# Program order on three engines, first loads in one queue by need, and a later router tail and x copy, in a gated linear-attention kernel

## The chip, the cores and the metric

The kernel runs on one core of one Trainium2 chip. The metric is device time in microseconds (us), lower is better. Times are medians of several executions. The granted TensorE clock of an execution is its mean over the span, 1 being full speed. In this kernel TensorE runs the matmuls (1510 instructions in the profile before), VectorE (278) and ScalarE (138) the element-wise work, POOL (GpSimd, 102) does small jobs and issues some copies, SP issues most copies (96 of 108 issues). PSUM is the memory that the matmuls write to; an evacuation takes a result out of it and frees its bank for the next matmuls (in the profile before, TensorE stood 2.85 us at the router for want of a bank). Warm-up matmuls are matmuls on zeros at the start, whose result is not used.

## The reference, cut to what matters

```python
qkv = x @ wqkv                                   # x: 2048 x 1024, wqkv: 1024 x 3072
pq, pk = phi(q), phi(k)                          # phi(t) = max(t,0) + min(exp(t),1) + 1e-6
kv, z = einsum(pk, v), pk.sum(rows)              # per head, 32 heads of 32
a = (pq @ kv / (pq @ z + 1e-6)) @ wo
r = x @ w_r; idx = argmax(r)                     # the router picks ONE row of x
y = (silu(x[idx] @ w_gate) * (x[idx] @ w_up)) @ w_down * sigmoid(r[idx])
b = x; b[idx] += y
g = sigmoid((x * gate_w).sum(-1))
out = g * a + (1 - g) * b
```

Nearly all work is dense projections. The one chain that is awkward is the router's: scores of all rows, the index of the largest, a fetch of that row from DRAM by a computed address, and a small feed-forward network on that one row, which is woven between the projections.

## The kernel before

The kernel is written in a framework that places instructions by a scheduler: the text of the program gives data dependences and rough priority, and the scheduler decides the order on each engine. The parts that the change and the argument touch (cuts marked with `# ...`):

```python
N_WARM = 8
load_x(0, 2); load_wkv(0); load_x(2, 2)          # tiles 0,1 ; first weight block ; tiles 2,3
# ... further weight blocks, transposed x, wq
nc.sync.dma_start(out=xp[:], in_=x2d)            # copy of x to a DRAM buffer that row idx will be patched in

def phi_evac(ps, out_ap):                        # evacuation of a PSUM bank; there are four
    nc.scalar.activation(e0[:], ps, ACTF.Exp)
    nc.vector.tensor_scalar(e1[:], e0[:], 1.0, EPS, op0=ALU.min, op1=ALU.add)
    nc.vector.scalar_tensor_tensor(out_ap, ps, 0.0, e1[:], op0=ALU.max, op1=ALU.add)
# ... router: scores, max, max_index on VectorE, then
nc.gpsimd.dma_start(out=c4[:], in_=cand[0:128:32, :])          # small copy across partitions
nc.vector.tensor_reduce(out=rmax[:], in_=c4[:, :, 0], ...)     # router tail: six small operations
# ...
idx_val = nc.values_load(idx_i[0:1, 0:1], engines=(POOL,), ...)
nc.gpsimd.dma_start(out=xsel_row[:], in_=x2d[bass.ds(idx_val, 1), :])   # the selected row
# ... in the feed-forward network, second half of the columns:
if nr < 4:
    nc.vector.memset(ps[96:128, :], 0.0)         # rows that no matmul of this half writes
# ... end of the key and value stage:
for i in range(3): nc.vector.tensor_copy(zcol[...], acc3[:, :, 128])
nc.vector.tensor_tensor(zc[:], mzc[:], zcol[...], op=ALU.mult)
for i in range(3): nc.vector.tensor_tensor(kvbd[...], acc3[...], mask_bd[...], op=ALU.mult)
rdA = den_group(0)                               # denominator: 16 matmuls on zc, banks freed by kvbd
```

## Time and profile before

| | before |
|---|---|
| median of 3 runs | 268.96 us (268.34 to 270.46) |
| profiled span | 267.3 us |
| TensorE busy | 255.7 us, 96% |
| idle in front of matmuls, summed | 8.2 us |
| mean granted clock, profiled run | 0.998 |

Three more from the page of the kernel before are needed later. The first is the granted clock in 40 equal slices of the span, in tenths, 9 being 90% or more. The other two are groups of instructions: line, engine, operation, count, then busy time, mean ns of one, and idle time before them.

```profile
PEclk9999999999999999999999999999999999999999
...
L195 PE MATMUL ps<-wkv,xT 128*128 128x512 bf16 x498 | 113.9, 379 | 2.2 <-DMA wkv<-in_A_wqkv_dram 1.0
...
L169 DVE TENSOR_SCALAR e<-e 128x512 f32<-128x512 f32 x64 | 31.4, 492 | 55.7 <-ACT e L167 55.5
```

After the start, where warm-up matmuls follow each other every 0.43 us and the clock records begin at 6.61 us, the clock stays at full speed (1.0 from 6.61 to 266.03 us) until the last matmul. The 379 ns of a projection matmul is the mean duration at that speed.

### The profile page before, as it was taken

Reading aid. Unit: us, or ns where it says so; the run is one execution under the profiler, and the core shown is the slowest. Engines: PE = TensorE matmul, PEld = TensorE weight load, DVE = VectorE, ACT = ScalarE, POOL = GpSimd, SP = SyncE. Lnnn points to the kernel's source line nnn. Section 1 sums busy time; section 2 is a strip of 40 time slices with the busy share of each in tenths; the row PEclk is TensorE's granted clock in tenths of the full one; section 3 lists DMA queues with packets and bytes.
Section 4 is the critical chain, followed back from the end, with each engine's and each line's share of the span. In section 5 each row is a group of like instructions: output and inputs, shape, how many; then the busy total and the mean of one; then the engine's idle time right before and its main releaser. Section 6 shows DMA issues by size and latency. Waiting matters only on the chain.

```text
span 267.3 us, 3972 instructions
## 1 busy us (share of the span) xinstructions
PE 255.7 (96%) x1510; PEld 121.8 (46%) x1537; DVE 144.5 (54%) x278; ACT 89.3 (33%) x138; POOL 50.3 (19%) x102
## 2 busy tenths in 40 slices
PE   7799999599999999999999999999999899999994
PEld 4444455245444445444444455544444344444443
DVE  4355014452375533539433425279999889984443
ACT  1433332123233322332322331233576623333310
POOL 7000001120000000000000000111969317990000
PEclk9999999999999999999999999999999999999999
DMA  6999998892078048019319608084000336455222
GB/s 228 359 312 220 246 521 306 292 415 93 0 259 333 1 154 316 4 45 348 120 36 357 238 0 300 17 286 168 1 1 2 125 100 197 150 170 177 86 78 78
DMA packets 33058, 47.71 MB, mean 178 GB/s; under 512 B 14152, under 2 KB 18640, under 8 KB 32976
## 3 DMA queue, kind: packets, MB, share of 16 engines
q1 hardware_dynamic: 32688, 47.32, 53.0%
q8 instruction: 12, 0.20, 0.3%
q0 software_dynamic: 320, 0.14, 0.2%
q14 instruction: 6, 0.05, 0.0%
q10 hardware_dynamic: 32, 0.00, 0.0%
HBM read 39.85 MB, written 8.39 MB: 180 GB/s over the span
## 4 chain that ended last, share of the span: by engine, by line
PE 77%; DVE 12%; DMA 7%; issue 2%; ACT 0%; POOL 0%; SPq 0%; DVEq 0%
PE ps L195 39%; PE ps L519 19%; PE ps L211 11%; DVE rb L476 4%; DVE e L169 3%; DMA c<-cand 3%; PE ps L320 3%; DVE pq_all L170 2%; DMA wkv<-in_A_wqkv_dram 2%; PE kvacc L204 2%; DMA rdp<-rd 1%; PE yps L359 1%; PE rps L237 1%; PE dps L453 1%; PE gl_ps L287 0%
## 5 line engine op out<-in xcount | busy, mean ns | idle before, releaser
L195 PE MATMUL ps<-wkv,xT 128*128 128x512 bf16 x498 | 113.9, 379 | 2.2 <-DMA wkv<-in_A_wqkv_dram 1.0
L195 PEld LDWEIGHTS <-xT 128*128 128x128 bf16 x512 | 48.8, 98 | 58.4 <-issue 2.9
L167 ACT ACTIVATE e<-ps 128x512 f32<-128x512 f32 x64 | 38.2, 597 | 81.7 <-PE ps L195 43.3
L169 DVE TENSOR_SCALAR e<-e 128x512 f32<-128x512 f32 x64 | 31.4, 492 | 55.7 <-ACT e L167 55.5
L211 PE MATMUL ps<-xT,wq 128*128 128x512 bf16 x248 | 58.3, 379 | 3.3 <-DVE idx_i L265 2.8
L519 PE MATMUL ps<-m_sb,pq_all 128*128 128x512 bf16 (+1 forms) x259 | 55.3, 372 | 1.0 <-DVE pq_all L170 0.6
L211 PEld LDWEIGHTS <-wq 128*128 128x128 bf16 x256 | 24.8, 98 | 33.6 <-issue 4.6
L519 PEld LDWEIGHTS <-pq_all 128*128 128x128 bf16 x264 | 25.7, 98 | 31.3 <-issue 1.8
L478 POOL TENSOR_TENSOR pq_all<-pq_all,rb 128x512 bf16<-128x512 bf16 x32 | 37.3, 1197 | 9.9 <-DVE rb L476 9.8
L200 ACT CAST vt<-ps 128x512 bf16<-128x512 f32 x32 | 18.8, 587 | 41.5 <-PE ps L195 41.5
L521 DVE SCALAR_TENSOR_TENSOR ot<-ps,gate,xg 128x512 bf16<-128x512 f32 (+1 forms) x33 | 23.8, 734 | 14.2 <-PE ps L519 14.1
L513 ACT ACTIVATE xg<-xt,omg 128x1024 f32<-128x1024 bf16 x16 | 18.2, 1151 | 29.7 <-DVE ot L521 25.0
L476 DVE STREAM_SHUFFLE rb<-rdp 128x512 f32<-128x512 f32 x32 | 22.7, 743 | 0.0
L170 DVE SCALAR_TENSOR_TENSOR pk<-ps,e 128x512 bf16<-128x512 f32 x32 | 22.1, 691 | 1.1
L170 DVE SCALAR_TENSOR_TENSOR pq_all<-ps,e 128x512 bf16<-128x512 f32 x32 | 21.8, 683 | 0.6
L192 POOL MEMSET vt<- 128x8 bf16 x16 | 1.9, 135 | 106.4 <-PE kvacc L204 106.4
L204 PEld LDWEIGHTS <-pk 128*128 128x128 bf16 x128 | 8.5, 98 | 3.3 <-issue 0.4
L204 PE MATMUL kvacc<-vt,pk 128*128 128x129 bf16 x128 | 9.7, 221 | 0.0
L484 ACT CAST m_sb<-ps 128x512 bf16<-128x512 f32 x16 | 8.6, 593 | 0.0
L458 DVE RECIPROCAL rd<-dn 128x512 f32<-128x512 f32 x2 | 6.7, 3353 | 3.2 <-ACT dn L456 3.2
L241 DVE CAST r_bf<-rps 128x512 bf16<-128x512 f32 x1 | 0.7, 691 | 13.9 <-PE rps L237 13.9
L365 POOL DMA_DIRECT2D xp<-brow x1 | 0.6, 575 | 38.5 <-DVE brow L364 38.5
(97 smaller groups left out, 87.0 us busy)
## 6 DMA issues: line engine op xcount, KB each, us to landing
wt<-in_B_w_down_dram SPq DMA_DIRECT2D x14, 512.0 KB, 9.2
wkv<-in_A_wqkv_dram SPq DMA_DIRECT2D x4, 1024.0 KB, 10.6
wt<-in_B_w_gate_dram SPq DMA_DIRECT2D x8, 512.0 KB, 21.6
wt<-in_B_w_up_dram SPq DMA_DIRECT2D x8, 512.0 KB, 8.1
xt<-xp SPq DMA_DIRECT2D x16, 256.0 KB, 2.7
out_dram<-ot SPq DMA_DIRECT2D x15, 256.0 KB, 2.0
wt<-in_B_w_gate_dram SPq DMA_DIRECT2D x8, 384.0 KB, 6.2
wt<-in_B_w_up_dram SPq DMA_DIRECT2D x8, 384.0 KB, 6.8
```

The source lines that it names most:

```text
L167: last_act[0] = nc.scalar.activation(e0[:], ps, ACTF.Exp)
L169: nc.vector.tensor_scalar(e1[:], e0[:], 1.0, EPS, op0=ALU.min, op1=ALU.add)
L170: nc.vector.scalar_tensor_tensor(out_ap, ps, 0.0, e1[:], op0=ALU.max, op1=ALU.add)
L195: nc.tensor.matmul(ps[:], lhsT=xT[:, c, t * P : (t + 1) * P], rhs=wkv[:, c, 512 * nb : 512 * nb + 512], start=(c == 0), stop=(c == KC - 1))
L200: nc.scalar.copy(vt_t[t][:, 4 * (nb - 2) : 4 * (nb - 2) + 4, 0:128], ps[:].rearrange("p (g e) -> p g e", g=4))
L204: nc.tensor.matmul(kv_slot(g), lhsT=pk_t[t][:, g * P : (g + 1) * P], rhs=vt_t[t][:, g, :], start=False, stop=False, skip_group_check=True)
L211: nc.tensor.matmul(ps[:], lhsT=wq[:, c, g * P : (g + 1) * P], rhs=xT[:, c, 512 * j : 512 * j + 512], start=(c == 0), stop=(c == KC - 1))
L476: nc.vector.stream_shuffle(rb[:], rd[:], [8 * (j % 2) + g] * 32)
L478: nc.gpsimd.tensor_tensor(sl, sl, rb[:], op=ALU.mult)
L513: pin_act(nc.scalar.activation(xg[:], xt[:], ACTF.Copy, scale=omg[:, t : t + 1]))
L519: nc.tensor.matmul(ps[:, 0:cw], lhsT=pq_all[:, g, t * P : (t + 1) * P], rhs=m_sb[:, g, c0 : c0 + cw], start=(g == 0), stop=(g == NG - 1))
L521: nc.vector.scalar_tensor_tensor(ot[:, c0 : c0 + cw], ps[:, 0:cw], gate[:, t : t + 1], xg[:, c0 : c0 + cw], op0=ALU.mult, op1=ALU.add)
```

## The change

The intent: fix the order by hand, so that a reduction that waits for a copy no longer stands in front of ready evacuations, and so that the first loads arrive in the order in which they are used. The core of the diff (cuts marked):

```diff
-N_WARM = 8
+N_WARM = 5
+    def in_order(engine, names):        # each instruction is pinned behind the last one on its engine
+        # ...
+    pe = in_order(nc.tensor, [...]);  dve = in_order(nc.vector, [...])
+    sp = in_order(nc.sync, [...]);    act = in_order(nc.scalar, [...])
# every nc.tensor / nc.vector / nc.scalar call below becomes pe / dve / act
-    load_x(0, 2)
-    load_wkv(0)
-    load_x(2, 2)
+    load_x(0, 1); load_w0(0); load_x(1, 1)
+    for c2 in range(1, 4): load_w0(c2)
+    load_x(2, 2)
# ...
-    nc.sync.dma_start(out=xp[:], in_=x2d)
# ... the matmuls of tiles 0 and 1 are interleaved in pieces as the loads arrive, then:
+    kv_mm(ps0, 0, 0, 6, 8); kv_evac(ps0, 0, 0)
+    kv_mm(ps1, 1, 0, 6, 8); kv_evac(ps1, 1, 0)
     for t in (2, 3): unit_T(t)          # tile 2's copy to SBUF now stands behind both evacuations
# ...
+    def router_part1():                 # the six small operations and POOL's copies
+        # ...
     ffn_prefetch()                      # the first ten weight loads of the feed-forward network
+    nc.sync.dma_start(out=xp[:], in_=x2d)
# ... in the loop over tiles, after the query units of tile t:
+        if t == 4:
+            router_part1()
```

## The prediction

Passages of the prediction are cut, and marked where they stood: they told rules of the hardware that no trace read for it had shown. None of them was a term of the sum, which stays as it was: 2.9 + 5.0 + 2.65 + 1.0 = 11.55 us, and 268.96 + 11.55 = 280.5 us. The sentence on ready evacuations stands on the profile before: VectorE stood for 5.91 us at the reduction, while an evacuation that ScalarE had finished with at 45.10 was taken up at 51.24. The matmul's drain of 0.16 us is the 1.89 us that eight matmuls take, less eight times 0.216.

> **What bounds the kernel now.** I read the page first, then the waits, then the timeline around each idle stretch of TensorE, and last the order in which the built program of the changed kernel puts its instructions on each engine.
>
> ```profile
> span 267.3 us, 3972 instructions
> PE 255.7 (96%) x1510; PEld 121.8 (46%) x1537; DVE 144.5 (54%) x278; ACT 89.3 (33%) x138; POOL 50.3 (19%) x102
> ...
> PE 77%; DVE 12%; DMA 7%; issue 2%; ACT 0%; POOL 0%; SPq 0%; DVEq 0%
> ```
>
> TensorE is busy for 255.7 of 267.3 us and is 77% of the chain that ended last. It leaves about 11.6 us, of which 8.2 us, summed over its instructions, are idle time in front of them and about 3 us the drain at the end. So the change can win little: at best the waits below. What it can lose is not so limited: every wait that it puts in front of a matmul costs its full length, since nothing else bounds. The waits of TensorE by their releaser:
>
> ```profile
> PE ps L211 <- DVE idx_i L265: 2.8, 1, 2.8
> ...
> PE warm_ps L217 <- DVE warm_sb L109: 1.4, 1, 1.4
> ...
> PE ps L195 <- DMA wkv<-in_A_wqkv_dram: 1.0, 1, 1.0
> ...
> PE ps L195 <- DVE xT L180: 0.6, 1, 0.6
> PE ps L519 <- DVE pq_all L170: 0.6, 1, 0.6
> ```
>
> The 2.8 us wait is the router. Timeline, columns start, duration, engine, line, operation, then the idle time before it:
>
> ```profile
> 42.39 0.72 POOL L255 DMA_DIRECT2D c<-cand  x1 [1.15 <-DVE cand L253]
> ...
> 50.54 0.14 DVE L257 TENSOR_REDUCE rmax<-c 1x1 f32<-1x4 f32 x1 [5.91 <-DMA c<-cand]
> ...
> 52.29 0.13 DVE L265 CAST idx_i<-idx_f 1x1 int32<-1x1 f32 x1
> ...
> 52.43 1.89 PE L211 MATMUL ps<-xT,wq 128*128 128x512 bf16 x8 [2.85 <-DVE idx_i L265]
> ...
> 58.42 0.54 POOL L268 DMA_DIRECT2D xsel_row<-in_A_x_dram  x1 [6.67 <-DVE pk L170]
> ```
>
> VectorE stands at the router's small copy for 5.91 us, does not empty PSUM, and TensorE runs out of its four work buffers. The copy needed 8.1 us because the packet records show the copy of x in 64 KB packets of about 2.9 us until 50.3; the small packets started at 47.7. Those 2.8 us are what the change aims at.
>
> [...]ready evacuations stood behind a waiting reduction. So an order is a commitment, and moving an instruction moves all behind it. [...]warm-up matmuls start 0.43 us apart, the first projections from 7.71 on 0.216 us[...].
>
> **The change part by part.** The order listing shows no arithmetic changed (three fewer warm-up matmuls); what changes is position. I followed each TensorE wait to the instruction that releases it and counted the matmuls between that instruction's own last input from TensorE and the waiting matmul. Zero means TensorE stands still for the whole chain. New zeros are at the start, at two memsets, and at the denominator.
>
> (1) Start. Loads arrive at about 0.18 MB per half microsecond (1.5 MB by 7.67). Tile 0 now lands at about 3.7 instead of 4.33, is transposed by 4.9, copied by 5.6, and the first projection starts near 5.7 instead of 7.71. But its pieces are interleaved with tile 1 and end only near 10.9 (0.6 before the old 11.5). Then strict order bites: VectorE's copy of the transposed tile 2 stands behind both evacuations. From exp at 11.0: 0.6, then two pairs of 0.43+0.69 less overlap, then 0.69 for the copy: near 14.1. Before, the copy went between:
>
> ```profile
> 12.02 0.69 DVE L180 COPY xT<-pst 128x1024 bf16<-128x1024 bf16 x1 [0.61 <-PE pst L176]
> ...
> 13.00 1.24 PE L195 MATMUL ps<-wkv,xT 128*128 128x512 bf16 x5 [0.57 <-DVE xT L180]
> ```
>
> So +1.1 us there (14.1 against 13.0)[...].
>
> (2) Router. The 2.85 us go: the tail now follows the second query unit, whose copy has landed by then. From 14.1, the same 36.6 us of matmuls bring that unit to 50.7 and its end to 52.5; its evacuation (0.6+0.43+0.69 with gaps, 1.9) and the six small operations (0.95) put the index at about 55.3, instead of 52.42. In the profile from the index to the landing of the selected row are 10.5 us (6.0 to POOL's issue, 4.5 to landing at 63.0). That gives 65.8. TensorE needs the row after 8.9 us of tile-5 work, at 61.3 (before: 63.35, after a wait of 0.42). New wait about 4.5 us; then xs_pad with no matmul to fill, 0.4 us. Position after this: 65.8 against 63.35, with the 0.4, +2.9 us against before; the 1.1 of (1) is contained in it, not added again. The copy of x now lies behind ten weight loads of 1.29 us (37.8+12.9, then 12.5 for itself: 50.7 to 63.2), across the row's own transfer, so this can be worse.
>
> (3) Two memsets of the padding rows of the second FFN half (0.485 us each). They stood early in VectorE's queue; now each follows the evacuation of the query unit just issued, and the FFN matmuls wait for it. Chain: matmul's drain 0.16, exp 0.60, e 0.43, the combine 0.69, memset 0.49, five hand-overs of about 0.03: 2.5 us, twice, +5.0.
>
> (4) Denominator. Before, the pieces of zcol and kvbd ran between evacuations, while 15 query matmuls ran:
>
> ```profile
> 172.72 3.40 PE L211 MATMUL ps<-xT,wq 128*128 128x512 bf16 x15
> ...
> 174.75 0.42 DVE L426 TENSOR_TENSOR zc<-mzc,zcol 128x256 bf16<-128x256 f32 x1
> ...
> 175.61 0.42 DVE L430 TENSOR_TENSOR kvbd<-kvacc,mask_bd 128x256 bf16<-128x256 f32 x1
> ...
> 176.09 1.05 PE L453 MATMUL dps<-pq_all,zc 128*32 128x512 bf16 x16
> ```
>
> The denominator matmuls wait for the last kvbd (176.03, then 176.09). Now only eight query matmuls (1.73 us) stand between, and VectorE first evacuates that unit. Chain: 0.16+0.6+0.43+0.69, zcol 3 x 0.155, zc 0.42, kvbd 0.55+0.55+0.42, less some overlap: 4.3 us of idle. The denominator ends at 172.72+1.73+4.3+1.05 = 179.8 instead of 177.15: +2.65, with seven query matmuls fewer behind it (1.5 us still to do).
>
> (5) End of the query stage. VectorE, from the arrival of the reciprocals, was full to the last evacuation:
>
> ```profile
> 186.24 0.73 DVE L476 STREAM_SHUFFLE rb<-rdp 128x512 f32<-128x512 f32 x1
> ...
> 208.59 1.89 PE L519 MATMUL ps<-m_sb,pq_all 128*128 128x512 bf16 x8 [0.56 <-DVE pq_all L170]
> ...
> 210.84 0.69 DVE L170 SCALAR_TENSOR_TENSOR pq_all<-ps,e 128x512 bf16<-128x512 f32 x1
> ```
>
> 25.3 us for 16 shuffles and 11 pairs, about 2.0 us per shuffle and pair. Strict alternation leaves 13 pairs behind the first shuffle: 9.1 us to the shuffle (186.24-177.15) plus 13 x 2.0 = 35.1 us after the denominator. TensorE comes to the second tile at 35.4 without that wait, and at about 36 with it; before it was 34.97 (212.12-177.15). +1.0 us. The remaining final stage has slack in both.
>
> Sum: 2.9 + 5.0 + 2.65 + 1.0 = 11.55; 268.96 + 11.55 = 280.5. Placing x's copy later and the strict queue of loads give nothing beyond (1): before, no matmul waits for a load after 7.71.
>
> **The rivals.** First, the intended one: the router's wait and the start are won and the rest is hidden. For it: 2.85+0.98+0.57 us are there to win. Against: wait chains of length zero are in the built program, and no other engine or work can fill them. It would give about 265. Second, the router only moves its wait and the memsets and denominator cost less than I sum, because operations overlap: 274 to 276. Third, a worse one: POOL's 4.6 us between having the address and issuing the row's copy grow under 64 KB packets, as the router's first copy took 8.1 us[...]: +3 to 5 us more, near 285. Fourth, VectorE becomes the bound of the query stage: at 2.2 instead of 2.0 us per pair step (5) costs 2.6 us more. A landed row without POOL's pause would be bounded by the end of x's copy, 63.2, and take 2 us off.
>
> **Range and chances.** Steps (3) and (4) are read from the program and from durations, 7.2 to 7.7 us; (1) with (2) I give -1 to +6, (5) 0 to 3.5. So 275.5 to 285.5 holds it 8 times in 10. Slower by over 2% begins at 274.3: 0.85; within 2%: 0.13; faster by over 2%: 0.02.
>
> **What would show it.** In the waits of the changed kernel: TensorE waiting for the memset twice, about 2.5 us each; for kvbd once, about 4.3; for the row's copy, about 4.5; none for idx_i. The projection of tile 2 starts near 14. The copy of x runs near 50.7 to 63.2. The idle sum of TensorE rises from 8.2 to about 21 us (11.55 more, and 1.3 for three warm-up matmuls that no longer count as busy). I am wrong if the memset waits are absent or below 1.5 us, if the row is in place before 62, or if the projection of tile 2 starts before 13.

## The result, and the profile after

| | before | after |
|---|---|---|
| median | 268.96 us | 284.77 us (281.72 to 286.34, 4 runs) |
| ratio of fast runs, 95% interval | | 1.054 [1.044, 1.064] |
| profiled span | 267.3 us | 282.8 us |
| TensorE busy | 255.7 us | 263.0 us |
| idle in front of matmuls, summed | 8.2 us | 16.6 us |
| mean granted clock of the runs | 0.991 to 1.0 over all groups | 0.964 to 0.987 |

A ratio is the mean time of one kernel's fast runs over that of the other kernel's fast runs in the same rounds, so it is not quite the ratio of the medians. One of the four runs after, 286.34 us at a clock of 0.964, counts as slow and is left out of the ratio. The change is slower by 15.8 us in the medians; the time lies inside the predicted range, near its upper end.

The page of the changed kernel, the same parts as before. All calls now go through one helper, so nearly all lines read L70 and one must go by the tile names.

```profile
span 282.8 us, 4003 instructions
...
PE 263.0 (93%) x1534; PEld 123.1 (44%) x1534; DVE 144.4 (51%) x278; ACT 89.3 (32%) x138; POOL 50.1 (18%) x102
...
PEclk9999999997999999988997999997999999999999
...
L70 DVE TENSOR_SCALAR e<-e 128x512 f32<-128x512 f32 x64 | 28.7, 449 | 80.1 <-ACT e L70 79.8
```

The second line shows that only part of the loss is idle time: TensorE has three warm-up matmuls fewer, yet it is *busy* 7.3 us longer. The third line shows most of why: four dips in the granted clock that the kernel before does not have. The clock records in the trace give four stretches at half speed, each 3.41 us long: 67.5 to 70.9, 125.5 to 128.9, 149.4 to 152.8 and 190.3 to 193.8. A window view (start and end, length, busy time and count of each engine, clock, DMA share, GB/s) of the first:

```profile
64.00:67.00 3.00, 1.17 (x16) 1.09 (x17) 0.69 (x2) 0.00 (x0) 1.38 (x4) 1.00 0.02 2
67.00:70.00 3.00, 3.00 (x11) 1.16 (x11) 0.60 (x3) 0.18 (x1) 0.00 (x0) 0.58 0.04 8
```

Before 67 TensorE is busy for 1.17 of 3 us; after it, it is fully busy and gets 11 instructions done at a mean clock of 0.58. Each dip goes with one of the new waits: three begin up to 2 us after the wait has ended, the fourth (190.34) inside it. The waits of TensorE, by releaser (total, count, longest):

```profile
PE ps L70 <- DVE ps L70: 5.0, 2, 2.5
...
PE dps L70 <- DVE kvbd L70: 3.8, 1, 3.8
...
PE ps L70 <- DVE xT L70: 3.0, 2, 2.2
...
PE xs_ps L70 <- DMA xsel_row<-in_A_x_dram: 2.8, 1, 2.8
```

The wait for `idx_i` is gone; these four have come. In the timeline (start, duration, engine, line, operation, idle before it and its releaser) the first is the start, tile 2:

```profile
14.07 0.68 DVE L70 COPY xT<-pst 128x1024 bf16<-128x1024 bf16 x1
14.81 1.04 PE L70 MATMUL ps<-wkv,xT 128*128 128x512 bf16 x4 [2.21 <-DVE xT L70]
```

The copy stood behind both evacuations, and tile 2 begins at 14.81 instead of 13.00. The router:

```profile
56.28 0.14 DVE L70 CAST idx_i<-idx_f 1x1 int32<-1x1 f32 x1
...
63.57 0.50 POOL L311 DMA_DIRECT2D xsel_row<-in_A_x_dram  x1 [7.29 <-issue]
65.47 0.35 PE L70 MATMUL xs_ps<-one_bf,xsel_row 1*128 1x1 bf16 x8 [2.80 <-DMA xsel_row<-in_A_x_dram]
66.17 1.05 PE L70 MATMUL gl_ps<-selg,rg_f 128*128 128x4 f32 x8 [0.35 <-DVE xs_pad L70]
```

From the index (56.42) to POOL's issue it took 7.15 us, against 6.0 before, and TensorE stood at the row. One of the two memsets:

```profile
123.89 0.48 DVE L70 MEMSET ps<- 32x512 f32 x1 [0.16 <-issue]
124.43 2.60 PE L70 MATMUL ps<-wt,xs_pad 128*32 128x512 bf16 x24 [2.52 <-DVE ps L70]
```

The memset itself is 0.48 us; the other 2 us are the evacuation in front of it. Its sister at 148.75 waited 2.46 us. The denominator:

```profile
185.35 1.89 PE L70 MATMUL ps<-xT,wq 128*128 128x512 bf16 x8
...
189.64 1.35 DVE L70 TENSOR_TENSOR kvbd<-kvacc,mask_bd 128x384 bf16<-128x384 f32 x3
191.04 1.90 PE L70 MATMUL dps<-pq_all,zc 128*32 128x512 bf16 x16 [3.80 <-DVE kvbd L70]
```

Besides the 3.80 us of idle, the same 16 matmuls last 1.90 us; before they lasted 1.05. That is the half clock: the window view gives 0.50 from 191.04 to 192.94, and 1.00 for these matmuls before. And the query stage behind it, in which VectorE alternates strictly between shuffle and evacuation:

```profile
201.99 0.72 DVE L70 STREAM_SHUFFLE rb<-rdp 128x512 f32<-128x512 f32 x1
...
203.67 0.72 DVE L70 STREAM_SHUFFLE rb<-rdp 128x512 f32<-128x512 f32 x1
```

The period is 1.68 us.

### The profile page after: what moved, and what is told of

It is laid out like the page before. It is cut to its first block, busy times and chain, and to the rows that moved or that the text cites. A ratio compares the mean times of both kernels' runs of the same rounds, so it can differ in the third digit from the quotient of the medians.

```text
span 282.8 us, 4003 instructions
## 1 busy us (share of the span) xinstructions
PE 263.0 (93%) x1534; PEld 123.1 (44%) x1534; DVE 144.4 (51%) x278; ACT 89.3 (32%) x138; POOL 50.1 (18%) x102
## 4 chain that ended last, share of the span: by engine, by line
PE 89%; DVE 5%; issue 3%; ACT 1%; DMA 1%; POOLq 0%; DVEq 0%
PE ps L70 81%; PE kvacc L70 3%; PE yps L70 1%; ACT e L70 1%; DVE e L70 1%; PE dps L70 1%; DVE pq_all L70 1%; PE warm_ps L70 1%; PE pst L70 1%; DMA xsel_row<-in_A_x_dram 1%; PE rps L70 1%; DVE pk L70 0%; DVE kvbd L70 0%; DVE xT L70 0%; PE gl_ps L70 0%
## 5 line engine op out<-in xcount | busy, mean ns | idle before, releaser
L70 PE MATMUL ps<-wkv,xT 128*128 128x512 bf16 x512 | 119.6, 389 | 3.2 <-DVE xT L70 3.0
L70 PEld LDWEIGHTS <-xT 128*128 128x128 bf16 x512 | 49.7, 100 | 64.6 <-issue 7.7
L70 DVE TENSOR_SCALAR e<-e 128x512 f32<-128x512 f32 x64 | 28.7, 449 | 80.1 <-ACT e L70 79.8
L70 ACT ACTIVATE e<-ps 128x512 f32<-128x512 f32 x64 | 38.1, 597 | 89.0 <-PE ps L70 87.9
L70 PE MATMUL ps<-xT,wq 128*128 128x512 bf16 x256 | 59.3, 381 | 0.0
L70 PE MATMUL ps<-m_sb,pq_all 128*128 128x512 bf16 (+1 forms) x264 | 55.6, 373 | 0.0
L70 PEld LDWEIGHTS <-pq_all 128*128 128x128 bf16 x264 | 25.8, 98 | 29.8 <-issue 0.4
L70 PEld LDWEIGHTS <-wq 128*128 128x128 bf16 x256 | 24.9, 98 | 30.6 <-issue 1.6
L70 ACT CAST vt<-ps 128x512 bf16<-128x512 f32 x32 | 18.8, 588 | 41.4 <-PE ps L70 41.4
L70 DVE SCALAR_TENSOR_TENSOR ot<-ps,gate,xg 128x512 bf16<-128x512 f32 (+1 forms) x33 | 23.9, 731 | 15.5 <-PE ps L70 13.5
L70 ACT ACTIVATE xg<-xt,omg 128x1024 f32<-128x1024 bf16 x16 | 18.2, 1147 | 25.9 <-DVE ot L70 25.9
L70 DVE SCALAR_TENSOR_TENSOR pk<-ps,e 128x512 bf16<-128x512 f32 x32 | 22.1, 692 | 1.2
L70 DVE SCALAR_TENSOR_TENSOR pq_all<-ps,e 128x512 bf16<-128x512 f32 x32 | 22.1, 692 | 1.1
L70 DVE STREAM_SHUFFLE rb<-rdp 128x512 f32<-128x512 f32 x32 | 22.4, 734 | 0.0
L70 PE MATMUL ps<-wt,xs_pad 128*32 128x512 bf16 x112 | 9.4, 438 | 5.0 <-DVE ps L70 5.0
L70 PEld LDWEIGHTS <-pk 128*128 128x128 bf16 x128 | 8.5, 98 | 3.3 <-issue 0.4
L70 PE MATMUL kvacc<-vt,pk 128*128 128x129 bf16 x128 | 9.7, 221 | 0.0
L70 DVE RECIPROCAL rd<-dn 128x512 f32<-128x512 f32 x2 | 6.7, 3353 | 3.8 <-ACT dn L70 3.8
L70 ACT CAST m_sb<-ps 128x512 bf16<-128x512 f32 x16 | 8.5, 591 | 0.0
```

The costliest lines, as they stand in the source:

```text
L70: inst = fn(*a, **k)
```

## The experiments

The theory after these readings: (a) VectorE's strict order puts chains of VectorE work in front of matmuls that have nothing else to run, which makes the waits at the memsets, the denominator and tile 2; (b) each idle stretch may drop the clock to one half for 3.41 us, which costs up to 1.7 us more and is the part that the sum of the prediction left out; (c) the row is late because the copy of x, in 64 KB packets, now runs across it. Rivals: the clock dips are scatter between runs; TensorE's own program order costs; POOL is late for another reason than the copy of x.

The twelve runs fall into three groups, each on one chip with its own runs of the kernel before: the first four below with 268.10 us, the next four with 268.31 us, the last four with 268.74 us. Across groups compare the ratios.

### The changed kernel again, in more rounds

No edit.

> The changed kernel once more, to see how its own time scatters. Theory (the clock falls to half for 3.4 us after idle stretches of TensorE, and how many stretches fall so differs from run to run): times scatter between about 281 and 287 us and rise with a falling mean clock, about 1.2 us for each 0.006 of mean clock (one fall). Rival (the scatter is something else, DMA for instance): times within 0.5% of each other, or no relation with the clock.

Measured: 284.77 us (283.60 to 285.75, 6 runs), ratio 1.060 [1.057, 1.064]; clock of the runs 0.964 to 0.976. Time goes with the clock: the three runs at 0.976 took 283.6 to 283.9 us, the three at 0.964 to 0.970 took 285.6 to 285.8. Idle at the row was 3.85 us this time, but the row's matmuls stood at 65.51, as at 65.47 in the first profile. Only three dips in this profile: after the row, the second memset and the denominator; the first memset, with the same 2.52 us of idle, had none. So a dip behind a 2.5 us wait comes often but not always: behind three of the four memset waits of these two profiles. Nor is its length fixed: in this profile the dips at the row and at the denominator last 6.83 us, twice 3.41.

### The memset out of the order

```diff
-    dve.memset(ps[96:128, :], 0.0)
+    nc.vector.memset(ps[96:128, :], 0.0)     # placed by the scheduler again
```

> Only the two memsets of the padding rows are left free to stand earlier on VectorE; all else as in the changed kernel. Theory: both idle stretches of 2.5 us before the FFN matmuls go, and with them two of the four falls of the clock (3.4 us at half speed, up to 1.7 us each): 6.5 to 8.5 us less, near 277. Rival (the idle time is only moved to the next wait): less than 3 us gained. Rival (the falls of the clock come anyway): 5 us gained, and four falls still there.

Measured: 276.46 us (274.28 to 276.85), ratio 1.027 [1.023, 1.032]: 8.3 us less than the changed kernel in the medians. Both memset waits are gone, and the profile has no dip in that part (two are left, at the row and at the denominator, the second 6.83 us long). The idle time taken away is 4.98 us. The other 3.3 us are what two dips at up to 1.7 us each would cost. Moving two instructions of 0.48 us recovers half of the loss.

### The memset waits kept, but filled with useless matmuls

```diff
+    keep_warm(11)                            # 11 matmuls on zeros, result unused
     dve.memset(ps[96:128, :], 0.0)
```

> The memsets stay late, but 11 matmuls of no use (0.216 us each, 2.4 us) stand in front of each of the two FFN blocks and fill the idle stretch. Theory (idle time is what lets the clock fall): the FFN matmuls start when they did, but the clock stays up at both places: 2 to 3.5 us less than the changed kernel in the same call, mean clock up by about 0.012. Rival (the clock falls for another reason): falls at the same places, time the same or up to 0.5 us longer.

Measured: 282.00 us (280.67 to 282.66), ratio 1.050 [1.047, 1.053], 2.8 us less, clock 0.976 to 0.988 against 0.964 to 0.976. TensorE does more work and the kernel is faster. The profile has no dip at the memsets. With the previous run this splits the 8.3 us: about 5 of waiting, about 3 of clock.

### The denominator's inputs before the last query units

```diff
     ffn_step(100)
-    unit_Q(*q_units.popleft())
     # zcol, zc, kvbd
+    for _ in range(2): unit_Q(*q_units.popleft())
     rdA = den_group(0)
-    unit_Q(*q_units.popleft())
```

> zcol, zc and kvbd are put right behind the last accumulation in program order, and two query units (instead of one) stand between it and the denominator, as the scheduler had it before. Theory: the 3.8 us of idle and the fall of the clock there go, and seven to eight query matmuls are no longer behind the denominator: 4 to 5.5 us less, near 280; VectorE still keeps up in the query stage. Rival (VectorE then becomes the bound of the query stage, as each unit there needs a shuffle and a pair): under 2.5 us gained and idle time of TensorE between 205 and 220 us.

Measured: 280.59 us (280.09 to 280.97), ratio 1.045 [1.041, 1.048], 4.2 us less. The wait at the denominator is gone; a new one of 1.32 us has come at 200.74, where a query unit waits for a bank that VectorE empties late. The profile shows four dips, none at the denominator; one, at 15.9, stands behind the wait for tile 2.

### POOL's small store behind the row

```diff
-    nc.gpsimd.dma_start(out=rmax_d[:], in_=rmax[0:1, 0:1])
+    store = nc.gpsimd.dma_start(out=rmax_d[:], in_=rmax[0:1, 0:1])
+    tc.add_manual_dep(store.ins, row.ins.name, NOSYNC, reason="store behind the row")
```

> In the changed kernel POOL has the row's address at 57.8 us but issues the row's copy only at 63.6. Here the store of the maximum, which POOL issues just before and which landed at 63.2, is issued behind the row's copy instead. Theory A ([...]an 8 KB packet of an instruction queue started at 61.9, as one did at 56.6 in the kernel before, 1.4 to 1.5 us ahead of the issue both times): the row's copy is still issued near 63.5, TensorE still waits 2 to 4 us, time within 1 us of 284.8. Theory B (the store in flight holds POOL up): the copy is issued near 58 and the wait is under 1 us; 3 to 5 us less.

Measured: 285.77 us (285.05 to 285.94), ratio 1.063 [1.058, 1.068]: no gain. In the timeline POOL had nothing in front of the row's copy and still issued it at the same moment:

```profile
63.49 0.49 POOL L311 DMA_DIRECT2D xsel_row<-in_A_x_dram  x1 [16.66 <-issue]
```

So POOL was not held up by its store. The packet records show what goes with the issue. They mark some packets on queue 14 as instruction packets (7 of them, 0.06 MB, on the page of the changed kernel). One such packet of 8 KB starts between 61.0 and 61.9 in this run, in the changed kernel and in its variants so far, about when the last 64 KB packets of the copy of x start (60.0 to 60.8), and POOL issues the row 1.7 to 2.2 us after it. That POOL waited for this packet, and the packet for the copy of x, was theory; these records show only the times. The next runs test the part that can be tested.

### The copy of x behind eight more loads

```diff
     ffn_prefetch()
-    nc.sync.dma_start(out=xp[:], in_=x2d)
# ... after the feed-forward step of tile 6:
+        if t == 6:
+            xcopy = nc.sync.dma_start(out=xp[:], in_=x2d)
+            tc.add_manual_dep(xcopy.ins, last_load[0].ins.name, NOSYNC, reason="copy of x behind these loads")
```

> The changed kernel with the copy of x moved behind the ten weight loads that tile 6 frees, past the router's transfers. Theory (the 64 KB packets of that copy hold up the router's small transfers[...]): POOL's pause falls from 5.8 to under 4.7 us, as under 4 KB packets or no traffic; the row is there before 63.0 and TensorE waits under 1 us for it, so no fall of the clock there: 3 to 4.5 us less, near 281. Rival (POOL's pause doesn't depend on the traffic): the row's wait stays above 2 us and the time within 1 us.

Measured: 282.24 us, but from 278.61 to 285.96 over 4 runs (the highest counted as slow); ratio 1.044 [1.036, 1.053]. (The edit puts the copy behind eight loads; the expectation's ten counts two too many.) The scatter follows the clock: 0.994, 0.982, 0.976, 0.964 for 278.6, 281.9, 282.6, 286.0. In the timeline:

```profile
60.29 0.50 POOL L311 DMA_DIRECT2D xsel_row<-in_A_x_dram  x1 [3.51 <-DVE pk L70]
...
65.15 1.86 PE L70 MATMUL gl_ps<-selg,rg_f 128*128 128x4 f32 x8 [1.69 <-DVE xs_pad L70]
```

The index stood at 56.91, so POOL took 3.4 us, and the row landed at 62.02, in time. Theory (c) holds: over all profiles of the strict kernels (all variants that keep VectorE in program order) with the copy of x in its first place, POOL issued at 63.0 to 63.8, with the index anywhere from 55.4 to 58.3, about when that copy ended (62.7 to 64.1); in the five runs with the later copy it issued 3.4 to 3.7 us after the index, with next to no other traffic (0.01 MB from 54 to 62 us in this run). What is not shown is that the 64 KB packets matter as such: in the kernel before, whose copy of x had landed at 50.3, POOL still took 6.0 us from the index and the row 4.5 us to land, under weight loads in 4 KB packets. In every one of the profiles, the kernel before among them, the issue stands 1.7 to 2.2 us behind an instruction packet on queue 14 (58.42 behind 56.56 in the kernel before, 63.57 behind 61.88 in the changed kernel); the packet comes early or late with the issue, and which of them holds the other is not shown. But most of the 2.80 us gained at the row came back as a 1.69 us wait one step later (it had been 0.35): the padded row's copy stands behind an evacuation on VectorE, and the wait at the row had hidden that. So the expected end of the dip at the row did not come either: one begins at 65.2 and lasts 6.83 us.

### The kernel before, with the later copy of x alone

The same move of the copy, in the kernel before; nothing else.

> The kernel before, with only the copy of x moved in the same way. Theory: the router's first small copy lands by about 47.5 instead of 50.5, VectorE stands at it for about 3 us instead of 5.9, TensorE's four buffers last, and the waits of 2.85 and 0.42 us go: 2.5 to 3.3 us less than before, near 265.3. Rival (another transfer or the row's wait takes its place): within 1 us of before.

Measured: 266.06 us (265.83 to 268.67, 6 runs), ratio 0.993 [0.988, 0.997], slightly faster than the kernel before. The router's wait that the change was made to remove is gone (VectorE waits 3.01 us for the small copy instead of 5.91, and TensorE not at all). The goal of the change could be had by moving one copy, without fixing any order.

### The changed kernel mended in four places

The free memset, the later copy and the early denominator as above, and tile 2's copy in front of the evacuations:

```diff
-    kv_evac(ps0, 0, 0)
     kv_mm(ps1, 1, 0, 6, 8)
+    unit_T(2)
+    kv_evac(ps0, 0, 0)
     kv_evac(ps1, 1, 0)
-    for t in (2, 3):
-        unit_T(t)
+    unit_T(3)
```

> The changed kernel with all four new waits taken away together: memsets free, denominator's inputs right behind the last accumulation, the copy of tile 2 ahead of the two evacuations, the copy of x later. Theory (the waits and their clock falls add up): 284.8 less 8.3 (memsets, measured) less 4.2 (denominator, measured) less 3 to 4.5 (row) less 1 to 2 (start): 265.5 to 268.5, about as the kernel before or up to 1% faster. Rival (the held order costs by itself): above 270.

Measured: 269.42 us (268.63 to 270.31), ratio 1.003 [0.999, 1.007]. Tile 2 starts at 12.40. All the large waits are gone; left are the 1.69 us for the padded row, with a dip right behind it at 63.2, and 1.38 us at 188.18. The loss of 5 to 6% is gone with these four edits together, though the expected 265.5 to 268.5 us was missed by 0.9 us.

### All three kinds of wait filled with useless matmuls

```diff
+    keep_warm(11)      # ahead of each memset
+    keep_warm(13)      # ahead of the matmuls on the selected row
+    keep_warm(17)      # ahead of the denominator
```

> The changed kernel with useless matmuls on zeros that fill most of three kinds of wait: 11 ahead of each of the two matmul blocks that wait for the memset, 13 ahead of the matmuls on the selected row, 17 ahead of the denominator. The waits themselves stay as long as they are; only TensorE is no longer idle in them. Theory (each idle stretch of about 2.5 us or more can drop the granted clock to one half for 3.42 us, which costs up to 1.7 us each): three to four clock falls go, mean granted clock about 0.99, time about 279 to 281, 4 to 5 us below the 284.8 of the changed kernel. Rival (the clock falls are noise and the lost time is the waits alone): within 0.7 us of 284.8, or above it where a filling overshoots its wait.

Measured: 278.48 us (278.29 to 279.27, 6 runs), ratio 1.035 [1.030, 1.040], clock 0.994 to 0.999. The clock line of its page:

```profile
PEclk9999999999999999999999999999999999999999
```

Fifty-two useless matmuls, over four places, and a gain of 6.3 us in the medians. The filled waits still hold TensorE up as before: the row's matmuls are at 65.64. This is the changed kernel with its waits and without its dips, so the dips cost about 6.3 us in the medians (6.9 us by the ratios, as the two kernels ran in different groups) and the waits the rest, 9 to 10 us. It also gained slightly more than was expected.

### VectorE placed by the scheduler, the rest of the change kept

```diff
-    dve = in_order(nc.vector, [...])
+    dve = nc.vector
```

The order on TensorE is the same, instruction by instruction, as in the changed kernel.

> The changed kernel, but VectorE's instructions are again placed by the scheduler; TensorE and ScalarE stay in program order, and the copy of x stays behind the first weight loads. TensorE's instruction order is identical to that of the changed kernel. Theory (VectorE's strict order alone makes the waits at the tile-2 copy, the two memsets and the denominator; the wait for the row belongs to the copy of x): no wait of TensorE for the memsets (2.52 and 2.46 before), none over 1.5 us at the denominator (3.80), the tile-2 projection near 12.4 rather than 14.8, but the row's matmuls still near 65.2, now after a longer wait of about 4 to 5 us, with one clock fall after it. Time about 271 to 274, some 12 us below 284.8 and 1 to 2% above the kernel before. Rival (TensorE's order carries the loss): above 280.

Measured: 275.09 us (272.99 to 275.42), ratio 1.020 [1.015, 1.026]: 9.7 us less than the changed kernel in the medians (10.6 by the ratios), though 1 us above the range that was expected. The memset waits are gone, tile 2 starts at 13.63 with an idle time of 0.42 us, and the denominator waits 1.48 us. So theory (a) holds for the bulk: with the same TensorE order, VectorE's order alone makes these waits. The row was expected near 65.2 and its matmuls stood at 63.88 after 2.35 us of idle: the index came 6 us earlier (50.53), POOL issued at 57.90, and then the row itself took 5.9 us from issue to landing, with the copy of x still running. In the other variants of the changed kernel that copy was out of the way or nearly done, and the row took 1.7 to 1.9 us.

### The same, with the later copy of x

> As the run with VectorE free, and the copy of x to DRAM placed behind the next eight weight loads (as in the two runs with the later copy). Theory: the row lands near 57 to 59, before TensorE wants it, no wait over 1.5 us is left anywhere and the clock stays at full speed: 265 to 267, so at or below the kernel before with the later copy (266.06), and the parts of the change that help (first loads by need, no reduction that stops VectorE) show for the first time, about 0.5 to 1 us. Rival (program order on TensorE itself costs): 268 or more.

Measured: 269.64 us (268.42 to 270.03), ratio 1.000 [0.995, 1.005], at full clock (1.0) in every run. The row is in time and there are no dips, but the expected 265 to 267 was missed; the number is the rival's. The trace shows two places. At the denominator 1.48 us of idle are left. And from the end of the first denominator group to that of the second it took 36.9 us, against 34.8 in the changed kernel and 34.8 in the kernel before: with VectorE free, the scheduler puts shuffles in front of ready evacuations, and TensorE waits for a bank.

```profile
202.97 0.72 DVE L523 STREAM_SHUFFLE rb<-rdp 128x512 f32<-128x512 f32 x1
203.10 1.89 PE L70 MATMUL ps<-xT,wq 128*128 128x512 bf16 x8 [1.24 <-DVE pq_all L182]
```

In this stage VectorE's operation on `e` also took 875 ns on average, as it took 837 in the kernel before and 547 in the changed kernel. So a fixed order on TensorE is not free when VectorE's order is not made to go with it. Which of the two places carries how much was not tried alone.

### The mended kernel, with the gate matmuls moved

```diff
# in router_part2: the gate logits become a part of their own, called later
+            if nb == 0 and t == 6:
+                router_gate()
```

> The mended kernel in strict order (free memset, tile-2 copy first, denominator early, copy of x later; 269.42), and in addition the matmuls of the gate logits moved behind the first key projection of tile 6, so that they no longer wait for the padded row, whose copy stands behind an evacuation on VectorE (1.69 us in the mended kernel, with a clock fall after it). Theory: that wait and the clock fall go: 1.7 plus up to 1.7 us, so 266 to 268. Rival (TensorE is held up by the same evacuation elsewhere, for the padded row is needed by the first feed-forward matmuls): about 269.

Measured: 267.08 us (265.45 to 268.00, 6 runs), ratio 0.992 [0.987, 0.997], about 2.3 us less than the mended kernel in the medians (3.0 by the ratios). The wait for the padded row is gone and its dip with it; of TensorE's waits only two are above 1.2 us:

```profile
PE warm_ps L70 <- DVE warm_sb L70: 1.4, 1, 1.4
PE ps L70 <- DVE pq_all L70: 1.2, 1, 1.2
```

Its stretch between the two denominator groups is 34.0 us, against 36.9 with VectorE free. So both kinds of order can reach the same place: this kernel and the kernel before with one copy moved have ratios of 0.992 and 0.993, both just faster than the kernel before. The 0.8% are measured against it in the same rounds; between the two there is no difference that these runs show.

## Why the prediction was right or wrong

By position on TensorE in the two profiles. Idle terms come from the timeline; a dip's cost is taken as half its length (granted clock 0.50 in the window view), as far as TensorE was busy in it.

| step of the prediction | predicted | measured |
|---|---|---|
| (1)+(2) position after the row and the padded row | +2.9 | +2.12 and 0.35, +2.5 |
| (3) two memsets | +5.0 | 2.52 + 2.46 = +5.0 |
| (4) denominator, without the dip | +2.65 | +2.3 |
| (5) end of the query stage, without the dip | +1.0 | -0.5 |
| clock dips | 0 in the sum | three of 1.7, and 1.3: +6.4 |
| sum | +11.55 | +15.7 |

How (4) and (5) are worked out: from the end of the last key and value matmul to the end of the denominator group it took 4.25 us before (172.88 to 177.13) and 7.42 after (185.51 to 192.93), of which 0.85 are the slow matmuls, so 7.42 - 0.85 - 4.25 = 2.3. From there to the end of the second group it took 34.83 and 34.76, of which 0.42 belong to the dip.

- **Right:** the direction, and that the loss comes from chains of VectorE work that TensorE cannot fill. Steps (3) and (4) have the size that was read from the built order and from durations of the kernel before. In (4) the terms add up to 4.29 us before any overlap, so none had been taken off; the idle time was 3.80. The experiments that took single waits away (memset, denominator, VectorE free) show the cause.
- **Right in sum, with terms that balance:** in step (2) the row's matmuls were put at 65.8 and came at 65.47, but the wait was 2.80 us and not 4.5: TensorE came there at 62.67 rather than 61.3, partly because tile 2 began at 14.81 and not at 14.1. A later TensorE makes the wait shorter by as much; the row sets the position. That the position came out is partly luck: the index came 1.1 us later than the 55.3 predicted, and from it to the landed row it took 9.0 us, not 10.5. All profiles of the strict kernel with the copy of x in that place have these matmuls between 64.8 and 65.6. So the start cost nothing of its own, as the prediction said in taking it as contained. To undo the start alone was not tried. Part of it is clock: in the second profile the clock rose to full speed at 5.2 us instead of 9.4, and tile 2 began at 13.79.
- **Wrong, step (5):** "Strict alternation leaves 13 pairs behind the first shuffle" at "about 2.0 us per shuffle and pair". The period measured 1.68 us. The 2.0 us had been taken from a stage in which the order was different and `e` took longer: 837 ns on average in this stage before, 547 after, and 410 in most of the strict periods. Why `e` takes longer in the one order is not shown. The strict order did not cost there; against a free VectorE on the same TensorE order it took 2 to 3 us less.
- **Wrong in size, the clock:** the sum had no term for it. Only the third rival counted on a fall of the clock, as an estimate of "+3 to 5 us more, near 285". In the profile after, the dips came with waits of 2.46 to 3.80 us, at four places. That is the mis-sized term: 6.4 us by the records of the first profile, 6.3 us by the run with filled waits. Without it the changed kernel would stand at 278.5, 2 us below the 280.5 of the sum; with it, at 284.8. The third rival's number came true, by a different count.
- **The forecast of idle time** (about 21 us) was too high; it was 16.6. The missing step (5) accounts for about 1.5 of the 4.4 us, the rest was not broken down. What the sum lacked stood in busy time, not in idle time.

**What goes with a dip.** It is not the length of one wait alone. At the 3.8 us wait at the denominator it came in 6 of the 6 profiles that had the wait unfilled. Behind the 2.5 us memset waits, it came in 7 of 10 cases (both in the first profile, one in the second, none with the later copy of x, both in two others). Behind the 2.0 to 2.4 us at tile 2 it came in two of eight. The kept traces show what separates the cases, when they are cut by their own clock records. In each of the 14 profiles all changes of the clock lie whole multiples of 3.413 us apart (to 2 ns), so in these profiles the clock changes on a grid of windows of that length. The grid does not start with the kernel: the first recorded change lies anywhere from 5.2 to 10.9 us (6.61 in the kernel before, 9.44 in the changed kernel). Up to the last matmul there are 1041 windows at full speed. The 23 that half speed follows hold at most 1.39 us of matmuls, the 1018 others at least 1.38, when the 1x1 and four-column matmuls at the row are not counted; without the windows that hold those, it is at most 1.22 against at least 1.38. All but one of the 23 had matmuls in them. So in these profiles a dip followed where a wait left less than about 1.3 us of one window to matmuls, an estimate from the 1.22 and the 1.38 us. In the first profile the four windows (from 64.05, 122.08, 145.97 and 186.93) keep 0.38, 1.06, 0.95 and 0.31 us, the other windows at full speed at least 1.45. There the first memset wait falls into the window from 122.08, which keeps 1.06 us of matmuls: a dip. In the second profile a window boundary at 124.64 cuts the same wait in two, and the windows keep 2.37 and 1.93 us: none. Half speed lasted one window in 17 cases and two in 6; in those 6 the first slow window held at most 2.57 us of such matmuls, in the 17 others at least 2.51. This was read after the runs; no run tested the limit by itself.

**What stays open.** ScalarE and SP kept program order in every variant of the changed kernel, so their part was not tested. That POOL waits for an instruction packet, and that packet for the copy of x, is not shown, only that their times go together; shown is that, with the changed order, the copy's place decides when the row comes (issue at 63.57 with the copy in its first place, at 60.29 with the later copy). What fills POOL's pause between the index and the issue of the copy that uses it as an address is open too: it was 3.4 to 3.7 us with the later copy of x, 4.8 to 8.4 us with that copy under way, and 6.0 us in the kernel before, under weight loads. The first 1.3 us of it, to the instruction that takes up the address, were the same in all profiles.

## What to carry to other kernels

When an order is fixed by hand, look for each matmul at what stands in front of its releaser on the other engine's queue, and count the TensorE work between them: zero meant here that the whole chain was paid, 2.52 and 2.46 us for two memsets of 0.48 us. On a TensorE-bound kernel like this one count an idle stretch of 2.5 us at about 1.5 times its length: a slow window came behind 7 of 10 of them here, at up to 1.7 us, so 2.5 + 0.7 x 1.7 = 3.7 us is the estimate from these runs. TensorE's busy time (263.0 against 255.7 us) and the clock line show this, the sum of idle time does not. Useless matmuls kept the clock up at the waits that they filled, in the profiles of both runs that tried them (clock of the runs 0.994 to 0.999 with all three kinds filled, 0.976 to 0.988 with the memset waits alone, 0.964 to 0.976 with none). Before reordering engines around one late transfer, try to move the large transfer that runs across it: moving the copy of x alone gave 266.06 us, against 268.31 before.
